# Wide tiles: the ring of weights' sums 64 bytes further, low parts ahead, both pairs of a step in a row, and four banks a pair

## The chip, the cores and the metric

The kernel runs on one core of a Trainium2 chip. The metric is the device time of one execution in microseconds; the median of three runs of the kernel before is 1164.0 us (1163.58 to 1164.37).

## The reference

Block-causal attention over 8 batches and 8 heads (sequence 576, head size 64, blocks of 64), and behind it a SwiGLU feed-forward on the 4608 tokens, all in float32:

```
scores = where(block_i >= block_j, (q @ k.T) / sqrt(64), -1e9)
x      = softmax(scores) @ v            # heads side by side: 4608 x 512
g      = x @ w_gate                     # 512 x 1536
val    = x @ w_val                      # 512 x 1536
out    = (g * sigmoid(g) * val) @ w_out # 1536 x 512
```

## The kernel before

**Precision.** A matmul's operands are float32 values split into a high and a low part. A product is three matmuls into one sum in PSUM: high by high, high by low, low by high.

**Order of the work.** The program first collects tasks (engine, cost in us, rank, buffers, what they wait for). A planner, `in_order()`, then plays them through on all engines at once with these costs and takes, whenever an engine is free, the task of least rank that is ready and finds a buffer slot. Slots whose tag is in `IN_TURN` are handed out in the order of the program. The order that comes out is the order of the instructions on every engine; what they wait for on the chip is set by the buffers that they share. Where the planner sees TensorE without work for over 0.3 us, `keep_busy` puts small filler matmuls there (64 columns, L1887 before, L1902 after).

**Stages.** Attention of the eight batches and the feed-forward of the finished tokens run next to each other. Twelve tiles of 256 tokens go the ordinary way: a step is gate and value products of two chunks of 128 hidden columns (48 matmuls of 128x256 at L1148: the gate's weights g_even and g_odd for the even and the odd chunk, the value's v_all), then twelve matmuls of 128x512 for the product with w_out (L1240 to L1242, "down").

**Wide tiles.** The last three tiles have 512 tokens each, from 870 us on. Gate and value products go by a scheme of seven products of half-size blocks in place of eight. A tile has six steps, each for two chunks: a gate `Pair` g and a value `Pair` v, both of 7 products of 6 matmuls of 128x256 (L1510). Products "1", "2" and "4" use the resident weights, "5", "6", "7" and "3" sums of weights, which `mix_weights` has worked out and stored in HBM (mix_d) during the attention. They are loaded from there into a ring of six slots in the buffer sc, four entries a pair, each entry by two DMAs of 128 KB (L1485, issued on SP's queue); an entry can be loaded once the product that used its slot is over. A pair's products stand in two PSUM tiles "at" of two banks each.

**Recombination.** ScalarE copies product "1" out of PSUM (s1, L1546); VectorE adds in four instructions at L1541: o1 (s1 to "2" and "6"), o2 ("7"), o3 ("5"), o4 ("3" and "4"). They write the pair's c, in the second sc buffer. Then `gates` (tanh on ScalarE, L1583; silu on VectorE, L1586) and `values` (product of gate and value on VectorE, L1599; its high part on ScalarE, L1602; its low part on VectorE, L1605). `bring` prepares the next tile's input blocks on VectorE and ScalarE meanwhile.

**Down chunks.** A step yields two chunks for `down` (12 matmuls of 128x512, L1628 to L1630, into the PSUM tiles po and gv, which add over a whole tile). They are put off: `owed` keeps them, and `give()` issues one of the previous step. So a step before reads: gate pair, gates, one down chunk of the step before, value pair, the other chunk, values.

## Time and profile before

| what | value |
|---|---|
| runs, median (lowest to highest) | 1164.0 us (1163.58 to 1164.37) |
| the profiled execution | 1164.27 us, span 1162.4 us, mean granted clock 0.993 |
| TensorE busy, 0 to 150 us | 142.84 of 150.00 us |
| TensorE busy, 150 to 870 us | 714.63 of 720.00 us |
| TensorE busy, 870 us to the end | 285.50 of 292.40 us |
| VectorE busy in these three | 122.73, 641.70 and 170.87 us |
| share of the DMA engines' time, 870 us to the end | 0.67, 211 GB/s |

A timeline row reads: start, how long the group lasted, engine, line, operation, output<-inputs by the program's names, tile shape, number of instructions, and in brackets the idle time before it and what ended that. A matmul's own duration (0.39 to 0.50 us) is longer than the distance to the next one, since matmuls are pipelined: what counts is the distance from start to start. A windows row gives the window, its length, busy time (and instructions) of PE, PEld (TensorE's weight loads), DVE (VectorE), ACT (ScalarE) and POOL, then the granted clock, the DMA share and GB/s. In the wide tiles the inputs' tiles carry the names of buffers that the attention no longer needs (qk, parts, mx, sr, xu, v, xhl).

### The profile page before, as it was taken

The numbers are of one execution on the slowest core, as the hardware profiler recorded it, in microseconds if no ns is written. First come the engines' busy times: TensorE is split into PE (matmuls) and PEld (weight loads), VectorE is DVE, ScalarE is ACT, GpSimd is POOL, SyncE is SP. The second block draws the span as 40 slices with busy tenths as digits, with TensorE's granted clock in tenths as the row PEclk, the third lists the DMA queues.
The fourth block names the chain that finished last, engine by engine and source line by source line (L and its number), as shares of the span: only waits on it lengthen the run. The fifth ranks groups of instructions, "written<-read, shape, count | busy, mean of one in ns | idle before, by whom it ended". The sixth has DMA issues, their size and how long they took to land.

```text
span 1162.4 us, 23307 instructions
## 1 busy us (share of the span) xinstructions
PE 1143.0 (98%) x8780; PEld 1008.5 (87%) x8780; DVE 935.3 (80%) x1540; ACT 580.2 (50%) x1052; POOL 324.7 (28%) x141
## 2 busy tenths in 40 slices
PE   8999999999999999999999999999999999999998
PEld 7778788889888888888888988988998999999996
DVE  4998898888898899998999999987665567556554
ACT  5889776755554465445565555554332224222222
POOL 3213101163644523454554345445100000000000
PEclk8999999999999999999999999999999999999999
DMA  7857766866666468767676668774577667766762
GB/s 193 225 147 210 198 189 229 214 186 183 151 191 168 142 186 222 202 188 203 195 190 184 179 176 239 203 216 159 177 226 246 220 205 232 226 205 222 241 209 99
DMA packets 328624, 228.97 MB, mean 197 GB/s; under 512 B 200064, under 2 KB 297616, under 8 KB 328512
## 3 DMA queue, kind: packets, MB, share of 16 engines
q1 hardware_dynamic: 325936, 226.77, 67.7%
q8 instruction: 69, 1.13, 0.4%
q10 hardware_dynamic: 2576, 0.72, 0.3%
q14 instruction: 43, 0.35, 0.1%
HBM read 190.45 MB, written 36.96 MB: 196 GB/s over the span
## 4 chain that ended last, share of the span: by engine, by line
PE 38%; DVE 10%; issue 2%; ACT 1%; POOL 1%; DMA 0%; DVEq 0%; ACTq 0%; POOLq 0%
PE at L1510 15%; PE gv L1148 8%; DVE mx L749 2%; DVE sc L779 2%; PE po L1240 2%; PE po L1241 1%; PE po L1242 1%; PE po L1628 1%; PE po L1629 1%; PE po L1630 1%; PE gv L1628 1%; PE gv L1629 1%; PE gv L1630 1%; PE at L861 1%; DVE hhl L1198 1%
## 5 line engine op out<-in xcount | busy, mean ns | idle before, releaser
L912 POOL PARTITION_ALL_REDUCE mx<-mx x48 | 181.1, 3826 | 183.8 <-DVE mx L749 175.8
L753 POOL PARTITION_ALL_REDUCE mx<-mx x80 | 143.1, 1832 | 305.9 <-DVE mx L749 191.7
L1148 PE MATMUL gv<-xhl,v_all 128*128 128x256 f32 x1728 | 221.1, 279 | 0.7 <-DVE t L1190 0.5
L1148 PEld LDWEIGHTS gv<-xhl,v_all 128*128 128x128 f32 x1728 | 208.2, 188 | 5.4 <-issue 1.9
L1541 DVE TENSOR_TENSOR sc<-sc,at 128x512 f32<-128x512 f32 (+1 forms) x144 | 89.3, 620 | 90.4 <-ACT sc L1546 53.5
L779 DVE TENSOR_TENSOR sc<-sc,mx 128x640 f32<-128x640 f32 (+6 forms) x168 | 127.1, 800 | 2.2 <-POOL mx L753 2.1
L749 DVE TENSOR_TENSOR mx<-mx,sc 128x128 f32<-128x128 f32 (+2 forms) x180 | 124.4, 703 | 1.5 <-ACT sc L783 0.3
L1148 PE MATMUL gv<-xhl,g_even 128*128 128x256 f32 x864 | 120.3, 284 | 2.0 <-DVE t L1185 2.0
L783 ACT ACTIVATE sc<-sc 128x1024 f32<-128x1024 f32 (+3 forms) x104 | 105.8, 1033 | 30.8 <-DVE sc L779 30.0
L1148 PEld LDWEIGHTS gv<-xhl,g_even 128*128 128x128 f32 x864 | 110.4, 189 | 8.8 <-DVE t L1185 2.2
L1148 PE MATMUL gv<-xhl,g_odd 128*128 128x256 f32 x864 | 115.8, 280 | 0.0
L1148 PEld LDWEIGHTS gv<-xhl,g_odd 128*128 128x128 f32 x864 | 107.2, 189 | 2.0 <-issue 1.2
L1240 PE MATMUL po<-wo,hhl 128*128 128x512 f32 x252 | 103.6, 411 | 0.7 <-ACT ob L1267 0.7
L1241 PE MATMUL po<-wo,hhl 128*128 128x512 f32 x252 | 98.8, 392 | 0.0
L1242 PE MATMUL po<-wo,hhl 128*128 128x512 f32 x252 | 98.5, 391 | 0.0
L861 PE MATMUL at<-sc,v 128*64 128x320 f32 (+4 forms) x888 | 94.3, 362 | 1.6 <-ACT parts L463 1.2
L709 ACT ACTIVATE sc<-at 128x576 f32<-128x576 f32 (+1 forms) x96 | 76.6, 835 | 31.5 <-PE at L692 31.4
L861 PEld LDWEIGHTS at<-sc,v 128*64 128x64 f32 x888 | 60.1, 137 | 36.1 <-ACT sc L783 2.0
L692 PE MATMUL at<-parts,qk 64*128 64x288 f32 (+4 forms) x864 | 73.9, 310 | 1.7 <-DVE qk L674 1.2
L692 PEld LDWEIGHTS at<-parts,qk 64*128 64x128 f32 x864 | 62.3, 185 | 14.7 <-issue 5.0
L1195 ACT CAST hhl<-t 128x512 fp32r<-128x512 f32 x72 | 44.8, 623 | 58.5 <-DVE t L1190 37.6
L1198 DVE TENSOR_TENSOR hhl<-t,hhl 128x512 fp32r<-128x512 f32 x72 | 62.7, 871 | 10.8 <-ACT hhl L1195 10.7
(238 smaller groups left out, 2037.3 us busy)
## 6 DMA issues: line engine op xcount, KB each, us to landing
wo<-wo_d SPq DMA_DIRECT2D x164, 512.0 KB
sc<-mix_d SPq DMA_DIRECT2D x288, 128.0 KB
mix_d<-wo SPq DMA_DIRECT2D x48, 256.0 KB
out_dram<-ob SPq DMA_DIRECT2D x35, 256.0 KB
v<-in_v_dram SPq DMA_DIRECT2D x64, 128.0 KB
rt<-r_d SPq DMA_DIRECT2D x128, 64.0 KB
qk<-in_q_dram SPq DMA_DIRECT2D x112, 72.0 KB
qk<-in_k_dram SPq DMA_DIRECT2D x104, 72.0 KB
```

The lines of the kernel that those rows point to most:

```text
L692: nc.tensor.matmul(ps[0][:, x, o : o + w], lhsT=part(1, kl)[own(x), c * P : (c + 1) * P], rhs=part(0, ql)[own(x), qs : qs + w], start=n == ...
L749: nc.vector.tensor_tensor(into, prev, of(c), op)
L753: nc.gpsimd.partition_all_reduce(m, m, channels=P, reduce_op=bass_isa.ReduceOp.max)
L779: nc.vector.tensor_tensor(piece(c), scores_of(c), m, ALU.subtract)
L783: nc.scalar.activation(x, x, AF.Exp)
L861: nc.tensor.matmul(ps[0][own(x), 1 - i if sums else i, q0 - s0 : s1 - s0], lhsT=ones if sums else vt[0][:, 2 * lane + c, own(x)], rhs=sc[0 ...
L912: nc.gpsimd.partition_all_reduce(m, m, channels=P, reduce_op=bass_isa.ReduceOp.add)
L1148: nc.tensor.matmul(o, lhsT=part[:, d], rhs=xs[d][1][x][:, 0:w], start=first, stop=last)
L1240: nc.tensor.matmul(po, lhsT=hi, rhs=whi, start=i + y == 0, stop=False)
L1241: nc.tensor.matmul(po, lhsT=hi, rhs=wlo, start=False, stop=False)
L1242: nc.tensor.matmul(po, lhsT=lo, rhs=whi, start=False, stop=i + y == NFC - 1)
L1510: nc.tensor.matmul(self.spot(name), lhsT=a, rhs=b, start=n == 0, stop=n == len(every) - 1)
```

## The change

1. The first sc buffer is 16 words longer, and the ring's views begin 16 words (64 bytes) further in it (`shifted`). The views that used the second sc buffer (`plain`, `four`) are written anew for its new shape; they hold the same bytes.
2. `product` takes several names. The gate's "12" issues its four matmuls of the low weights first, then the eight of the high ones.
3. A pair's order is "12", "6", "75", "34" in place of "15", "26", "7", "34", and the ring's entries come in the order 6, 7, 5, 3. The four banks of a pair are four `Part`s ("bank") of the two PSUM tiles, handed out in turn.
4. In a step, `v.issue()` stands ahead of the first `give()`: gate pair, value pair, then both down chunks.
5. In `mix_weights` the sums for the value weights are one VectorE instruction of 128x512 in place of two of 128x256 (twelve times), and the planner is given that cost.

```diff
--- before.py
+++ after.py
@@ -301,7 +301,7 @@
-    pool_of(const, "sc", 2, now=([([P, 2, WS], F32)], None), late=([([P, 6, 2 * XT], F32R)], None))
+    pool_of(const, "sc", 2, now=([([P, 2, WS], F32)], None), late=([([P, 6 * 2 * XT + 16], F32R)], None))
@@ -1287,8 +1287,12 @@
 
                 def whole(which=which, i=i, c=c, sums=sums):
                     to = sums[0].rearrange("p (d y f) -> p d y f", d=2, y=2)
+                    if which:
+                        hi, lo = (v_all[x][:, c::2, i * P : (i + 2) * P].bitcast(F32) for x in range(2))
+                        nc.vector.tensor_tensor(to.rearrange("p d y f -> p d (y f)"), hi, lo, ALU.add)
+                        return
                     for y in range(2):
-                        hi, lo = (w_at(which, x, i + y)[:, c :: 2].bitcast(F32) for x in range(2))
+                        hi, lo = (w_at(which, x, i + y)[:, c::2].bitcast(F32) for x in range(2))
                         nc.vector.tensor_tensor(to[:, :, y], hi, lo, ALU.add)
 
                 def mixes(sums=sums):
@@ -1312,7 +1316,7 @@
-                t = add("DVE", 2 * dve_us(2 * P), R, whole, [*w_done.values(), *early], [sums, mix], True)
+                t = add("DVE", dve_us(DM) if which else 2 * dve_us(2 * P), R, whole, [*w_done.values(), *early], [sums, mix], True)
@@ -1333,7 +1337,11 @@
         def cut(b, k, x):
             return b, lambda b: (b[x][:, k, 0:w], b[x][:, k, w:W])
 
-        sc = [cut(b, k, 0) for b in parent["sc"] for k in range(6)]
+        def shifted(b, k):
+            at = 16 + k * W
+            return b, lambda b: (b[0][:, at : at + w], b[0][:, at + w : at + W])
+
+        sc = [shifted(parent["sc"][0], k) for k in range(6)]
@@ -1347,17 +1355,17 @@
...
+        ats = [Buf("at") for _ in range(2)]
+        banks = [(b, lambda b, k=k: b[0][:, k]) for b in ats for k in range(2)]
+        slots["bank"] = [[None, None] for _ in banks]
         RING = 6
         AT = {"5": 3, "6": 0, "7": 1, "3": 2}
         slots["ring"] = [[None, None] for _ in range(RING)]
@@ -1473,11 +1481,11 @@
             def __init__(self, j, i, which, xs, ready, E, rank):
                 self.E, self.rank, self.i, self.which = E, rank, i, which
                 self.xs, self.ready = xs, ready
-                self.ps = [Buf("at") for _ in range(2)]
+                self.ps = [Part("bank", banks) for _ in range(4)]
                 self.c = Part("value" if which else "gate", four[which : which + 1])
                 n, stored = mixed[which, i]
                 self.ring, self.loads = {}, {}
-                for name in "5673":
+                for name in "6753":
                     x = Part("ring", sc[0:RING])
 
                     def load(n=n, b=AT[name], x=x):
@@ -1489,34 +1497,42 @@
                     self.ring[name] = x
                     self.loads[name] = dma(E, 2.6e5, load, stored, [x], 2)
 
-            def product(self, name, low_first=False):
-                hw, lw = {}, {}
-                which, i = self.which, self.i
-                for c in range(2):
-                    if name in "124":
-                        y, d = {"1": (0, c), "2": (0, 2 + c), "4": (1, 2 + c)}[name]
-                        hw[c], lw[c] = (w_at(which, x, i + y)[:, d] for x in range(2))
-                    else:
-                        v = self.ring[name].view()
-                        hw[c], lw[c] = (v[x][:, c * P : (c + 1) * P] for x in range(2))
-                x = [self.xs[XN[name], c].view() for c in range(2)]
-                every = [[(lw[c], x[c][0]), (hw[c], x[c][0]), (hw[c], x[c][1])] for c in range(2)]
+            def product(self, names, low_first=False):
+                every = []
+                for name in names:
+                    which, i = self.which, self.i
+                    some, o = [], self.spot(name)
+                    for c in range(2):
+                        if name in "124":
+                            y, d = {"1": (0, c), "2": (0, 2 + c), "4": (1, 2 + c)}[name]
+                            hi, lo = (w_at(which, x, i + y)[:, d] for x in range(2))
+                        else:
+                            hi, lo = (v[:, c * P : (c + 1) * P] for v in self.ring[name].view())
+                        x = self.xs[XN[name], c].view()
+                        some.append([(o, lo, x[0]), (o, hi, x[0]), (o, hi, x[1])])
+                    every.append(some)
                 if low_first:
-                    every = [[a for a, _, _ in every]] + [[b, c] for _, b, c in every]
+                    order = [three[0] for some in every for three in some]
+                    order += [p for some in every for three in some for p in three[1:]]
                 else:
-                    every = [[b, c, a] for a, b, c in every]
-                every = sum(every, [])
-                for n, (a, b) in enumerate(every):
-                    nc.tensor.matmul(self.spot(name), lhsT=a, rhs=b, start=n == 0, stop=n == len(every) - 1)
+                    order = [three[k] for some in every for three in some for k in (1, 2, 0)]
+                left, seen = {}, set()
+                for o, _, _ in order:
+                    left[id(o)] = left.get(id(o), 0) + 1
+                for o, a, b in order:
+                    left[id(o)] -= 1
+                    nc.tensor.matmul(o, lhsT=a, rhs=b, start=id(o) not in seen, stop=not left[id(o)])
+                    seen.add(id(o))
 
             def spot(self, name):
-                k, bank, o = {
-                    "1": (0, 0, 0), "5": (0, 0, 1), "2": (0, 1, 0), "6": (0, 1, 1), "7": (1, 0, 0), "3": (1, 1, 0), "4": (1, 1, 1)
-                }[name]
-                return self.ps[k][0][:, bank, o * w : (o + 1) * w]
+                k, o = {"1": (0, 0), "2": (1, 0), "6": (1, 1), "7": (2, 0), "5": (2, 1), "3": (3, 0), "4": (3, 1)}[name]
+                return self.ps[k].view()[:, o * w : (o + 1) * w]
+
+            def pair_of(self, k):
+                return self.ps[k].view().rearrange("p (k n) -> p k n", k=2)
 
             def on_pe(self, names):
-                bufs, after = [self.ps["734".find(names[0]) >= 0]], []
+                bufs, after = [*dict.fromkeys(self.ps[{"1": 0, "2": 1, "6": 1, "7": 2, "5": 2}.get(n, 3)] for n in names)], []
                 for name in names:
                     bufs += [self.xs[XN[name], c] for c in range(2)]
                     after += [self.ready[XN[name], c] for c in range(2)]
@@ -1525,18 +1541,17 @@
                         after.append(self.loads[name])
 
                 def products():
-                    for name in names:
-                        self.product(name, name == "1" and not self.which)
+                    self.product(names, "1" in names and not self.which)
 
                 return on_pe(up_us(6 * len(names)), self.rank, products, bufs, after=after, stage="up")
 
...
-                t15 = self.on_pe("15")
-                s1 = add("ACT", act_us(w, True), E, out_of_psum, [t15], [p0, c])
-                self.t = t26 = self.on_pe("26")
+                self.t = t12 = self.on_pe("12")
+                s1 = add("ACT", act_us(w, True), E, out_of_psum, [t12], [pa, c])
+                t6 = self.on_pe("6")
                 o1 = op(
-                    W, [t26, s1], [p0],
+                    W, [t6, s1], [pb],
                     lambda: c.view()[:, 0:2],
                     lambda: c.view()[:, 2:3].to_broadcast([P, 2, w]),
-                    lambda: p0[0][:, 1].rearrange("p (k n) -> p k n", k=2),
+                    lambda: self.pair_of(1),
                 )
-                t7 = self.on_pe("7")
-                o2 = op(w, [t7, o1], [p1], lambda: at(2), lambda: at(1), lambda: self.spot("7"))
+                t75 = self.on_pe("75")
+                o2 = op(w, [t75, o1], [pc], lambda: at(2), lambda: at(1), lambda: self.spot("7"))
                 o3 = op(
-                    W, [o2, t15], [p0],
+                    W, [o2], [pc],
                     lambda: c.view()[:, 1::2],
                     lambda: c.view()[:, 1:3],
                     lambda: self.spot("5").rearrange("p (k n) -> p k n", k=1).to_broadcast([P, 2, w]),
                 )
                 t34 = self.on_pe("34")
                 o4 = op(
-                    W, [t34, o3], [p1],
+                    W, [t34, o3], [pd],
                     lambda: c.view()[:, 1:3],
                     lambda: c.view()[:, 1:3],
-                    lambda: p1[0][:, 1].rearrange("p (k n) -> p k n", k=2),
+                    lambda: self.pair_of(3),
                 )
                 self.done = [o3, o4]
@@ -1684,8 +1699,8 @@
                     chain["down"] = []
                     first[0] = False
                 before = gates(g)
+                v.issue()
                 give()
-                v.issue()
                 give()
                 hidden = values(v, before)
@@ -1758,7 +1773,7 @@
 
 
     IN_TURN = set(
-        "qk v parts sc mx xu sr gv hhl t xt rt xhl ring gate value plain".split()
+        "qk v parts sc mx xu sr gv hhl t xt rt xhl ring gate value plain bank".split()
     )
 
     def in_order():
```

TensorE at the start of a gate pair in the third tile, first before, then after (g_even_73 is the low part, g_even_72 the high part, sc the ring, at_0_161 and at_0_213 the two PSUM tiles):

```order
L1630 MATMUL gv_0_189<-wo_0_2044,hhl_1_108 128x512
L1510 MATMUL at_0_161<-qk_0_8859,g_even_73 128x256 x2
L1510 MATMUL at_0_161<-qk_0_8859,g_even_72 128x256 x4
L1510 MATMUL at_0_161<-qk_0_8977,sc_0_8653 128x256 x6
L1510 MATMUL at_0_161<-qk_0_8859,g_even_72 128x256 x2
L1510 MATMUL at_0_161<-qk_0_8859,g_even_73 128x256
L1510 MATMUL at_0_161<-qk_0_8977,g_even_72 128x256 x2
L1510 MATMUL at_0_161<-qk_0_8977,g_even_73 128x256
L1510 MATMUL at_0_161<-parts_0_9000,sc_0_8653 128x256 x3
L1510 MATMUL at_0_161<-parts_1_9001,sc_0_8653 128x256 x3
```

```order
L1645 MATMUL gv_0_189<-wo_0_2044,hhl_1_108 128x512
L1524 MATMUL at_0_161<-qk_0_8857,g_even_73 128x256 x3
L1524 MATMUL at_0_161<-qk_0_8978,g_even_73 128x256
L1524 MATMUL at_0_161<-qk_0_8857,g_even_72 128x256 x6
L1524 MATMUL at_0_161<-qk_0_8978,g_even_72 128x256 x2
L1524 MATMUL at_0_161<-parts_0_8989,sc_0_8626 128x256 x3
L1524 MATMUL at_0_161<-parts_1_8990,sc_0_8626 128x256 x3
L1524 MATMUL at_0_213<-parts_0_8960,sc_0_8626 128x256 x3
L1524 MATMUL at_0_213<-parts_1_8961,sc_0_8626 128x256 x3
L1524 MATMUL at_0_213<-qk_0_8978,sc_0_8626 128x256 x6
```

The four matmuls of the low part stand together at the start, and no ring product stands between "1" and "2".

TensorE where that gate pair ends, before and after:

```order
L1510 MATMUL at_0_213<-mx_0_8953,sc_0_8653 128x256 x6
L1510 MATMUL at_0_213<-mx_0_9009,g_odd_68 128x256 x2
L1510 MATMUL at_0_213<-mx_0_9009,g_odd_69 128x256
L1510 MATMUL at_0_213<-mx_0_9009,g_odd_68 128x256 x2
L1510 MATMUL at_0_213<-mx_0_9009,g_odd_69 128x256
L1628 MATMUL po_0_262<-wo_0_2083,hhl_0_109 128x512
L1629 MATMUL po_0_262<-wo_0_2083,hhl_0_109 128x512
```

```order
L1524 MATMUL at_0_213<-mx_0_8941,sc_0_8626 128x256 x6
L1524 MATMUL at_0_213<-mx_0_9009,g_odd_68 128x256 x2
L1524 MATMUL at_0_213<-mx_0_9009,g_odd_69 128x256
L1524 MATMUL at_0_213<-mx_0_9009,g_odd_68 128x256 x2
L1524 MATMUL at_0_213<-mx_0_9009,g_odd_69 128x256
L1524 MATMUL at_0_161<-qk_0_8857,v_all_70 128x256 x2
L1524 MATMUL at_0_161<-qk_0_8857,v_all_71 128x256
L1524 MATMUL at_0_161<-qk_0_8857,v_all_70 128x256 x2
```

Before, the down chunk follows the gate pair; now the value pair does (v_all). It takes 18 matmuls ("12" and "6") until the tile at_0_213 is written again.

In the second step of the second and of the third tile the value pair's last two groups stand like this on TensorE after the change (the ring products are "75", then "34"):

```order
L1524 MATMUL at_0_213<-parts_0_8960,sc_0_8626 128x256 x3
L1524 MATMUL at_0_213<-parts_1_8961,sc_0_8626 128x256 x3
L1524 MATMUL at_0_213<-qk_0_8978,sc_0_8626 128x256 x6
L1902 MATMUL po_0_262<-ones 64x64 x4
L1524 MATMUL at_0_213<-mx_0_8941,sc_0_8626 128x256 x6
L1524 MATMUL at_0_213<-mx_0_9009,v_all_70 128x256 x2
L1524 MATMUL at_0_213<-mx_0_9009,v_all_71 128x256
```

Four filler matmuls stand ahead of "34". On VectorE in the second step of the second tile, before (L1586 is the gate's silu, L1541 o1 to o4 of the value pair, L1599 its product with the gate) and after (L1601 the silu, L1556 o1 to o4 of the value pair):

```order
L1586 SCALAR_TENSOR_TENSOR t_0_111<-t_0_111,sc_0_8840 128x512 [waits Activation_49]
L1586 SCALAR_TENSOR_TENSOR t_0_977<-t_0_977,sc_0_8840 128x512 [waits Activation_49]
L1541 TENSOR_TENSOR sc_0_8840<-sc_0_8840,at_0_161 128x512 [waits Activation_49]
L1541 TENSOR_TENSOR sc_0_8840<-sc_0_8840,at_0_213 128x256 [waits DVE_49,PE_49]
L1541 TENSOR_TENSOR sc_0_8840<-sc_0_8840,at_0_161 128x2x256 [waits DVE_49]
L1541 TENSOR_TENSOR sc_0_8840<-sc_0_8840,at_0_213 128x512 [waits DVE_49]
L1599 SCALAR_TENSOR_TENSOR t_0_111<-t_0_111,sc_0_8840 128x512 [waits DVE_49]
```

```order
L1601 SCALAR_TENSOR_TENSOR t_0_111<-t_0_111,sc_0_8825 128x512 [waits Activation_49]
L1601 SCALAR_TENSOR_TENSOR t_0_977<-t_0_977,sc_0_8825 128x512 [waits Activation_49]
L1556 TENSOR_TENSOR sc_0_8825<-sc_0_8825,at_0_161 128x512 [waits Activation_49]
L1556 TENSOR_TENSOR sc_0_8825<-sc_0_8825,at_0_213 128x256 [waits DVE_49,PE_49]
L1556 TENSOR_TENSOR sc_0_8825<-sc_0_8825,at_0_213 128x2x256 [waits DVE_49]
L1556 TENSOR_TENSOR sc_0_8825<-sc_0_8825,at_0_213 128x512 [waits DVE_49,PE_49]
```

In these two steps o4 of the value pair has a wait for TensorE of its own beside that of o2, where in the other steps o2 alone waits, for the pair's last matmul: here o2 and o3 stand ahead of "34" in the program, and all three work on at_0_213. They also stand behind the two silus.

13 lines of the change are left out of this document (5 added, 8 removed).

## The prediction

> **What bounds the kernel now.** I read the busy shares first, then the windows, then what TensorE waits for in the wide stage.
>
> ```profile
> PE 1143.0 (98%) x8780; PEld 1008.5 (87%) x8780; DVE 935.3 (80%) x1540; ACT 580.2 (50%) x1052; POOL 324.7 (28%) x141
> 870.00:1162.40 292.40, 285.50 (x1978) 264.84 (x1976) 170.87 (x287) 69.52 (x138) 0.00 (x0) 1.00 0.67 211
> 150.00:870.00 720.00, 714.63 (x5601) 630.01 (x5600) 641.70 (x1008) 390.12 (x685) 287.52 (x101) 1.00 0.68 192
> PE at L1510 <- DVE sc L1541: 1.3, 1, 1.3
> ```
>
> TensorE is busy 98% of the span. In the wide stage (870 us to the end) the granted clock is 1.00 (the figure ahead of the DMA share) and the one wait for the recombination is 1.3 us long, the last row. So the stage's time is the sum of TensorE's intervals from start to start, and there are two ways to change it: shorter intervals, or new waits. VectorE is busy 171 of 292 us there and is not the bound, but its chains end waits.
>
> One step of the wide stage is a gate pair (42 matmuls at L1510), a down chunk (12 at L1628 to L1630), a value pair and a second down chunk. TensorE's timeline of one step:
>
> ```profile
> 1042.58 0.86 PE L1510 MATMUL at<-xhl,g_even 128*128 128x256 f32 x6
> ...
> 1047.54 0.40 PE L1628 MATMUL po<-wo,hhl 128*128 128x512 f32 x1
> ...
> 1050.29 0.87 PE L1510 MATMUL at<-xhl,v_all 128*128 128x256 f32 x6
> 1050.99 0.87 PE L1510 MATMUL at<-xhl,sc 128*128 128x256 f32 x6
> ...
> 1053.84 0.88 PE L1510 MATMUL at<-v,sc 128*128 128x256 f32 x6
> 1054.56 0.84 PE L1510 MATMUL at<-xu,v_all 128*128 128x256 f32 x6
> 1055.24 0.40 PE L1628 MATMUL po<-wo,hhl 128*128 128x512 f32 x1
> ```
>
> From start to start the gate pair takes 4.96 us, the down chunk 2.75, the value pair 4.95: with the second chunk, 15.41 us a step. The product from the ring ("sc") that starts at 1053.84 takes 0.72 for six, 120 ns each; the last one from the resident weights v_all takes 0.68, 113 ns. Both have the same shape, so the place of the weights matters. In the allocation of the built kernel the ring lies at multiples of 128 bytes, as do the moving operands; v_all, g_odd and the high parts of g_even lie 64 bytes beside such multiples, and g_even's low part on them.
>
> An ordinary step before the wide stage has the same 128x256 matmuls without a ring:
>
> ```profile
> 837.73 1.54 PE L1148 MATMUL gv<-xhl,g_even 128*128 128x256 f32 x12
> 839.11 1.52 PE L1148 MATMUL gv<-xhl,g_odd 128*128 128x256 f32 x12
> 840.47 2.88 PE L1148 MATMUL gv<-xhl,v_all 128*128 128x256 f32 x24
> 843.19 0.40 PE L1240 MATMUL po<-wo,hhl 128*128 128x512 f32 x1
> ```
>
> The 24 of v_all take 2.72 us, 113.3 ns each. The g_even group, whose four low parts go first, takes 1.38 for 12, 0.02 over 12 times 113.3, and nothing is written to g_even in that time. I read the ring's 120 ns as a matter of address and not of the transfers that fill it.
>
> **The change, part by part.** *The ring's shift and the low parts first.* If all ring products run at 113.3 ns, a value pair takes 42 x 0.1133 = 4.76 us and a gate pair, with the 0.02 for its low parts, 4.78. The step becomes 4.78 + 4.76 + 2 x 2.75 = 15.04 us against 15.41: 0.37 less, times 18 steps, **6.7 us gained**. Bounds: at best the same; at worst only the resident products gain, and the 24 ring products of 36 pairs keep their 120 ns: 24 x 36 x 0.0067 = 5.8 us of the gain are gone. I take the full gain, since g_odd and v_all, 64 bytes off, show it. In the Trainium skill, "SBUF — State Buffer", section "Who interferes with whom", TensorE has one read port for the moving operand and another, independent one for the weights, and waits on nobody. By that rule the shift would gain nothing, and the sum would be 5.8 us higher. The 0.72 against 0.68 us of the rows shows that equal matmuls do differ with the weights' place, so I follow the row.
>
> *The order "12", "6", "75", "34", both pairs in a row.* No matmul is added. But the value pair now stands right behind the gate pair, with no down chunk between them, and its "75" goes into the PSUM tile of two banks from which VectorE has yet to take the gate's products 7, 5, 3 and 4. The four banks are parts of two tiles, and the built program's waits go by tile: "75" of the value pair waits for the last addition (o4) of the gate pair, and the first addition into that tile (o2) waits for the gate's last matmul. What that chain takes is in the trace, in the chain that ended last and in the timeline near the end:
>
> ```profile
> 886.50 0.43 DVE sc L1541
> 886.96 0.70 DVE sc L1541
> 887.65 0.14 issue
> 887.79 3.81 PE at L1510 x30
> ...
> 1147.00 0.84 PE L1510 MATMUL at<-mx,v_all 128*128 128x256 f32 x6
> 1147.68 0.40 PE L1628 MATMUL po<-wo,hhl 128*128 128x512 f32 x1
> 1147.88 1.87 DVE L1541 TENSOR_TENSOR sc<-sc,at 128x256 f32<-128x256 f32 x3 [1.03 <-PE at L1510]
> ```
>
> The last matmul of a pair starts 0.11 before 1147.68, at 1147.57; o2 starts at 1147.88, 0.31 later; o2, o3 and o4 take 1.87; from the end of an addition to the matmul that it releases pass 0.14 us (887.65 to 887.79). Together 2.32 us. Meanwhile TensorE has "12" and "6" of the value pair: from the gate's last matmul to the start of "75" 19 intervals of 113.3 ns, 2.15 us. It stands for 0.17 us. A wait also has an aftermath:
>
> ```profile
> 656.24 3.09 PE L1148 MATMUL gv<-xhl,v_all 128*128 128x256 f32 x24 [0.54 <-DVE t L1190]
> 659.25 1.02 PE L692 MATMUL at<-parts,qk 64*128 64x448 f32 x10
> ```
>
> These 24 matmuls after a wait take 3.01 us where the 24 at 840.47 took 2.72: 0.29 more. Part of that may lie in the passage to the other matmuls at 659.25, so I take 0.2. Each such wait then costs 0.37 us. There is one in each of 18 steps, and one more at the start of the first tile, whose first step has no down chunks behind it: 19 x 0.37 = **7.0 us lost**. Bounds: 0, if the additions are over sooner than these rows say by 0.17 us; and 19 x (0.17 + 0.29) = 8.7. I take 7.0, since the two rows for the chain agree to 0.01 us. Behind the waiting "75" stand "34" and both down chunks; nobody else waits for them, since the down chunks' results go out only at a tile's end.
>
> *Two longer waits.* In the value pairs of the second step of the second and the third tile, the order sets o2 and o3 of that same pair ahead of its "34", in the same tile: "34" has to wait for o3, and o3 stands on VectorE behind the gate's silu (L1586). The rows for that:
>
> ```profile
> 894.34 1.41 DVE L1541 TENSOR_TENSOR sc<-sc,at 128x512 f32<-128x512 f32 x2
> 895.84 1.15 ACT L1583 ACTIVATE t<-sc 128x512 f32<-128x512 f32 x2 [3.47 <-DVE sc L1541]
> 896.50 1.30 DVE L1586 SCALAR_TENSOR_TENSOR t<-t,sc 128x512 f32<-128x512 f32 x2 [0.76 <-ACT t L1583]
> L1541 DVE TENSOR_TENSOR sc<-sc,at x144: 415/686/690, 876.4 to 1149.1; 128x512 f32<-128x512 f32 x108, 128x256 f32<-128x256 f32 x36
> ```
>
> o4 of a gate ends at 894.34 + 1.41 = 895.75 and the two silus at 896.50 + 1.30 = 897.80, 2.05 later. Then o1, o2, o3: 0.69 + 0.42 + 0.69 with three times 0.02 between, 1.86, and 0.14 to the matmul: "34" starts 4.05 us after o4 of the gate. Without that wait it would start after 0.14 and the twelve matmuls of "75" at 117 ns and the slow start, some 1.6 us. So 2.4 us of standing and 0.1 for the new start, 2.5 us, twice: **5.0 us lost**. Bounds: 2.0 and 3.0 each.
>
> *What goes away.* The wait at 887.79 and the small ones behind the last value pair:
>
> ```profile
> 885.62 0.84 PE L1510 MATMUL at<-mx,v_all 128*128 128x256 f32 x6
> 887.79 0.94 PE L1510 MATMUL at<-qk,g_even 128*128 128x256 f32 x6 [1.33 <-DVE sc L1541]
> ...
> 1150.20 0.39 PE L1630 MATMUL gv<-wo,hhl 128*128 128x512 f32 x1
> ...
> 1152.24 0.39 PE L1628 MATMUL po<-wo,hhl 128*128 128x512 f32 x1
> ```
>
> The six at 885.62 need 0.68 and the next would start at 886.30, not 887.79: 1.5 us gained, as that gate's "12" writes a tile that is free by then. At the end, the matmul at 1152.24 is the fourth after 1150.20 + 0.23, so without waits it would start at 1151.12: 1.1 us gained, because two down chunks, 5.5 us, now lie between the last value pair and the chunks that need its result, where one chunk of 2.75 lay. **2.6 us gained.**
>
> *The sums of weights.* Twelve pairs of 128x256 additions become twelve of 128x512, and the planner, given another duration, sets the attention's matmuls in another order from the middle of the attention on. The windows bound it:
>
> ```profile
> 500.00:700.00 200.00, 197.48 (x1577) 173.30 (x1574) 191.68 (x297) 108.99 (x190) 94.63 (x33) 1.00 0.70 190
> ```
>
> VectorE is nearly full there (191.68 of 200), but TensorE too (197.48), and over 150 to 870 us TensorE idles 5.4 us in all. The twelve instructions saved are worth little while TensorE stays full; the new order may win some of those 5.4 us or add to them. I count nothing, with 2 us either way, a third of them and a little more.
>
> **Sum.** -6.7 + 7.0 + 5.0 - 2.6 = +2.7 us. The profiled execution took 1164.27 us (1162.4 of span and 1.9 around it), 0.27 above the median of the runs, 1164.0. So the forecast is 1164.0 + 2.7 = **1166.7 us**.
>
> **The rivals.** *A, the waits cost next to nothing.* If the additions finish 0.17 us sooner, or "75" starts 0.17 us later because "12" and "6" still run at 117 to 120 ns, the stops and their aftermath vanish: 7.0 us less, 1159.7 us, faster. For it: 0.17 us is a small difference of two sums of 2.2. Against it: what lengthens "12" and "6" takes as much from the gain. *B, the two long waits are absent or short.* That takes 5.0 us off, 1161.7 us or, with half of them, 1164.2: no change. Against it: they are in the order of the instructions. *C, the ring's products stay at 120 ns.* Then 5.8 us of the gain are lost; "12" and "6" take 6 x 0.0067 = 0.04 longer, which shortens 19 waits to 0.33: 0.8 back, 1171.7 us, slower. For it: the transfers that fill the ring go on next to it, in both kernels; against it: g_even's row. It is also what the Trainium skill's rule of two ports (page and section above) comes to. *D, the ring runs dry.* Entries 3 and 4 of a value pair now reuse the slots of the gate's first two, 48 matmuls or 5.4 us ahead, where a down chunk lay between. The stage moves 211 GB/s at a DMA share of 0.67, and a pair's entries are 1 MB, so it should hold; if each third entry came 0.5 us late in 18 steps, 9 us more, 1175.7. *E, the earlier order.* 2 us either way on top of any of them.
>
> **How the numbers follow.** I give the forecast, with its own range 1164.5 to 1169, 0.45; A 0.2; B 0.2; C 0.1; D 0.05. 0.2% of 1164.0 is 2.3 us, about what a measurement of this kernel can tell from no change. Slower (over 1166.3): 0.29 of the forecast's cases, C, D and 0.01 of B, 0.45. The same: 0.16 of the forecast, 0.14 of B and 0.05 of A, 0.35. Faster (under 1161.7): 0.15 of A and 0.05 of B, 0.20. The range reaches down to A's 1159.7 and up to the forecast with the upper price of the waits and the earlier order against it, 1166.7 + 1.7 + 1.5: 1159.5 to 1170.
>
> **What would show it.** In TensorE's waits from 870 us on, 19 new entries of L1524 for VectorE's L1556 of about 0.1 to 0.2 us, and two of over 2 us. In a step, six ring matmuls in 0.68 us where 0.72 stood, and after the short wait 0.70 to 0.71. No idle row near 887 and none after the last value pair. The wide stage starting within 2 us of where it did, near 870 us. The forecast is wrong if L1556 is missing among the waits (A), if only the two long ones are missing (B), if ring products still take 0.72 (C), if a wait names the transfer sc<-mix_d (D), or if the stage starts further off (E).

## The result, and the profile after

The changed kernel took **1175.65 us** (median of four runs, 1174.48 to 1177.83) where the kernel before took 1164.18: a ratio of 1.0101 (95% interval 1.0084 to 1.0119), 11.5 us slower. The forecast was 1166.7 us in a range of 1159.5 to 1170: the right sign, and far too small.

The profiled execution (1177.83 us, span 1176.0) tells at once that most of it did not happen in the wide stage. TensorE's timeline there begins with the first of these rows (columns: start, length, engine, line, tiles, count); before, the stage began at 870.56 us.

```profile
882.18 1.54 PE L1524 MATMUL at<-qk,g_even 128*128 128x256 f32 x12
```

So 11.62 us were lost ahead of the wide stage, and the stage itself took 1176.02 - 882.18 = 293.84 us in place of 291.88: 1.96 more. (Their sum, 13.6, is 2 us above the difference of the medians, since the profiled execution was the slowest of the four.) The windows of the changed kernel that answer to those shown of before (busy us of PE, PEld, DVE, ACT, POOL, then granted clock, DMA share, GB/s):

```profile
150.00:870.00 720.00, 705.50 (x5527) 620.87 (x5526) 635.66 (x979) 387.62 (x679) 288.09 (x101) 1.00 0.67 189
500.00:700.00 200.00, 192.52 (x1518) 169.81 (x1517) 189.55 (x279) 106.67 (x186) 87.55 (x31) 0.98 0.66 183
```

TensorE's idle time between 150 and 870 us grew from 5.4 to 14.5 us, and the granted clock of 500 to 700 us fell to 0.98. What TensorE waited for, from 150 to 870 us (first two rows) and from 870 us on (last two):

```profile
PE gv L1148 <- DVE t L1185: 8.8, 4, 4.9
PE at L861 <- ACT sc L721: 2.5, 2, 1.6
...
PE at L1524 <- DVE sc L1556: 3.1, 2, 1.6
PE at L1524 <- DMA sc<-mix_d: 2.0, 2, 1.1
```

L1185 is the silu of the ordinary tiles on VectorE; the next gate product needs the PSUM bank that it reads. Before, all waits for it came to 2.0 us. The longest one now is 4.9 us. VectorE and GpSimd around it:

```profile
520.31 0.94 DVE L1310 TENSOR_TENSOR wo<-ob,wo 128x512 fp32r<-128x512 f32 x1
521.17 0.28 DVE L1301 TENSOR_TENSOR ob<-ob 128x128 f32<-128x128 f32 x1
521.49 2.69 DVE L1302 TENSOR_TENSOR ob<-ob 128x128 f32<-128x128 f32 x1
524.22 0.29 DVE L1303 TENSOR_TENSOR ob<-ob 128x128 f32<-128x128 f32 x1
524.54 0.29 DVE L1304 TENSOR_TENSOR ob<-ob 128x128 f32<-128x128 f32 x1
524.75 0.68 DVE L1185 SCALAR_TENSOR_TENSOR t<-t,gv 128x512 f32<-128x512 f32 x1
525.54 0.69 DVE L1190 SCALAR_TENSOR_TENSOR t<-t,gv 128x512 f32<-128x512 f32 x1
526.14 2.08 DVE L674 TENSOR_TENSOR qk<-sr,qk 128x576 fp32r<-128x576 f32 x1
...
521.43 7.25 POOL L912 PARTITION_ALL_REDUCE mx<-mx  x2
```

L1301 to L1304 are the additions of `mix_weights`. They stand ahead of the silu, and the second one takes 2.69 us in place of 0.29, from the moment that GpSimd's all-reduce starts. The same place in the kernel before:

```profile
516.88 0.64 DVE L1185 SCALAR_TENSOR_TENSOR t<-t,gv 128x512 f32<-128x512 f32 x1
...
521.05 0.29 DVE L1298 TENSOR_TENSOR ob<-ob 128x128 f32<-128x128 f32 x1
521.37 2.50 DVE L1299 TENSOR_TENSOR ob<-ob 128x128 f32<-128x128 f32 x1
...
521.12 7.25 POOL L912 PARTITION_ALL_REDUCE mx<-mx  x2
```

There an addition is held up just as long, but the silu is over by then. The wait also has a price of its own behind it (a window of the changed kernel, and TensorE's timeline):

```profile
526.00:531.50 5.50, 5.50 (x28) 5.50 (x27) 2.83 (x3) 0.49 (x1) 4.65 (x2) 0.50 0.64 189
```

```profile
525.49 2.93 PE L1148 MATMUL gv<-xhl,g_even 128*128 128x256 f32 x12 [4.91 <-DVE t L1185]
528.21 2.76 PE L1148 MATMUL gv<-xhl,g_odd 128*128 128x256 f32 x12
530.77 3.32 PE L1148 MATMUL gv<-xhl,v_all 128*128 128x256 f32 x24
534.02 1.06 PE L692 MATMUL at<-parts,qk 64*128 64x288 f32 x12
```

The granted clock is 0.50 up to 531.5 us. From start to start the twelve g_even products take 2.72 us where the step before the change that the prediction shows at 837.73 took 1.38, the g_odd ones 2.56 where it took 1.36, and the 24 of v_all, most of them at the full clock again, 3.25 where it took 2.72: about another 3 us. The Trainium skill says in "TensorE: Matmul & The Clock Gate", Part 1, that a stretch of about 3.4 us without work halves TensorE's clock until it has worked as long again. The wait of 4.91 us and the 0.50 agree with it; the half clock lasted longer here, 6.0 us of work, and a run below has it behind a wait of only 2.70 us.

In the wide stage, one step of the third tile after the change:

```profile
1071.27 1.54 PE L1524 MATMUL at<-qk,g_even 128*128 128x256 f32 x12
...
1076.05 1.52 PE L1524 MATMUL at<-qk,v_all 128*128 128x256 f32 x12
1077.41 1.73 PE L1524 MATMUL at<-parts,sc 128*128 128x256 f32 x12
1078.98 0.84 PE L1524 MATMUL at<-qk,sc 128*128 128x256 f32 x6
1079.66 0.84 PE L1524 MATMUL at<-mx,sc 128*128 128x256 f32 x6
...
1081.02 0.40 PE L1643 MATMUL po<-wo,hhl 128*128 128x512 f32 x1
...
1086.49 0.40 PE L1524 MATMUL at<-qk,g_even 128*128 128x256 f32 x2
```

Six ring products take 0.68 us (1078.98 to 1079.66) where they took 0.72. The gate pair takes 4.78 us. The row of twelve at 1077.41 is "6" and "7" of the value pair (the profile joins them, since their inputs have the same names); it takes 1.57 us where twelve products need 1.36. The step takes 15.22 us, 15.21 in most steps. From the starts of the gate pairs, the steps of the wide stage:

| step | before, us | after, us |
|---|---|---|
| first of the first tile | 17.23 | 15.25 |
| second of the first tile | 16.10 | 17.47 |
| first of the second tile | 15.42 | 16.91 |
| second of the second and of the third tile | 15.41 | 17.69, 17.75 |
| the other twelve | 15.41 | 15.21 (two 15.31) |
| the last, up to the start of the last matmul | 21.78 | 20.41 |

The two rows of 17.7 are the two long waits. The second of the first and the first of the second tile contain a wait for the ring's transfers (2.0 us in the two by the view of waits).

### The profile page after: what moved, and what is told of

Its sections match the earlier page's. It is cut to its first block, busy times and chain, and to the rows that moved or that the text cites. A ratio compares the mean times of both kernels' runs of the same rounds, so it can differ in the third digit from the quotient of the medians.

```text
span 1176.0 us, 23325 instructions
## 1 busy us (share of the span) xinstructions
PE 1142.5 (97%) x8796; PEld 1006.1 (86%) x8796; DVE 935.8 (80%) x1528; ACT 578.3 (49%) x1052; POOL 325.3 (28%) x141
## 4 chain that ended last, share of the span: by engine, by line
PE 74%; DVE 15%; DMA 4%; ACT 3%; issue 2%; SPq 1%; POOL 1%; DVEq 0%; ACTq 0%
PE gv L1148 25%; PE at L1524 14%; PE at L861 7%; PE po L1240 4%; PE at L692 4%; PE po L1241 4%; PE po L1242 4%; DVE mx L749 2%; DVE sc L779 2%; PE po L1644 1%; PE po L1643 1%; PE po L1645 1%; PE gv L1644 1%; DVE hhl L1198 1%; PE gv L1645 1%
## 5 line engine op out<-in xcount | busy, mean ns | idle before, releaser
L1148 PE MATMUL gv<-xhl,v_all 128*128 128x256 f32 x1728 | 221.4, 279 | 1.9 <-DVE t L1190 1.8
L1148 PEld LDWEIGHTS gv<-xhl,v_all 128*128 128x128 f32 x1728 | 208.6, 188 | 6.5 <-DVE t L1190 2.7
L1556 DVE TENSOR_TENSOR sc<-sc,at 128x512 f32<-128x512 f32 (+1 forms) x144 | 89.2, 620 | 67.5 <-PE at L1524 43.0
L1148 PE MATMUL gv<-xhl,g_even 128*128 128x256 f32 x864 | 121.5, 285 | 8.9 <-DVE t L1185 8.8
L779 DVE TENSOR_TENSOR sc<-sc,mx 128x640 f32<-128x640 f32 (+6 forms) x168 | 123.7, 779 | 5.2 <-POOL mx L753 5.2
L1148 PEld LDWEIGHTS gv<-xhl,g_even 128*128 128x128 f32 x864 | 111.0, 190 | 16.7 <-DVE t L1185 10.3
L749 DVE TENSOR_TENSOR mx<-mx,sc 128x128 f32<-128x128 f32 (+2 forms) x180 | 117.8, 669 | 1.3
L1148 PE MATMUL gv<-xhl,g_odd 128*128 128x256 f32 x864 | 116.0, 280 | 0.0
L1148 PEld LDWEIGHTS gv<-xhl,g_odd 128*128 128x128 f32 x864 | 107.3, 190 | 2.0 <-issue 1.2
L709 ACT ACTIVATE sc<-at 128x576 f32<-128x576 f32 (+1 forms) x96 | 76.5, 836 | 32.5 <-PE at L692 32.4
L1198 DVE TENSOR_TENSOR hhl<-t,hhl 128x512 fp32r<-128x512 f32 x72 | 69.9, 970 | 14.6 <-ACT hhl L1195 14.5
L692 PE MATMUL at<-parts,qk 64*128 64x288 f32 (+4 forms) x864 | 73.8, 310 | 0.6 <-DVE qk L674 0.5
L692 PEld LDWEIGHTS at<-parts,qk 64*128 64x128 f32 x864 | 62.2, 185 | 12.8 <-issue 3.5
L1617 ACT CAST hhl<-t 128x512 fp32r<-128x512 f32 x36 | 22.4, 622 | 101.3 <-DVE t L1614 60.2
```

What stands on the lines that cost most here:

```text
L692: nc.tensor.matmul(ps[0][:, x, o : o + w], lhsT=part(1, kl)[own(x), c * P : (c + 1) * P], rhs=part(0, ql)[own(x), qs : qs + w], start=n == ...
L749: nc.vector.tensor_tensor(into, prev, of(c), op)
L779: nc.vector.tensor_tensor(piece(c), scores_of(c), m, ALU.subtract)
L1148: nc.tensor.matmul(o, lhsT=part[:, d], rhs=xs[d][1][x][:, 0:w], start=first, stop=last)
```

## The experiments

Theory O says that the loss ahead of the wide stage comes from the order that the planner made of the new cost of the sums; rival W, that the wide tiles' edits disturb what is ahead of them. Theory S says that the wide stage gained by the shift and lost by its new waits.

**The parts of the change alone.** First the changed kernel with the old sums of weights:

```diff
-                    if which:
-                        hi, lo = ...  # one addition of 128x512
-                        return
...
-                t = add("DVE", dve_us(DM) if which else 2 * dve_us(2 * P), R, whole, ...
+                t = add("DVE", 2 * dve_us(2 * P), R, whole, ...
```

> The changed kernel with the sums of weights as before (two additions of 128x256, and the planner's old cost for them); the wide tiles as changed. Theory O (the new order of the attention's matmuls, which the planner made from the new cost, took most of the loss): the wide stage starts near 870.6 us as before, the wide stage keeps its +2.0 us, so about 1166.2 us (1165 to 1167.5). Rival W (the wide tiles' edits, their buffers or their slots disturb the stages ahead): still about 1175.

Measured: 1166.09 us, ratio to before 1.0024 (1.0009 to 1.0038). Then the other way round, the kernel before with the new sums and their cost, and nothing else:

> The kernel before with only the sums of weights changed (one addition of 128x512 and its cost). Theory O: it loses what the changed kernel lost ahead of the wide stage, 9 to 12 us: about 1174 us, with a wait of about 5 us of L1148 for VectorE near 520 us. Rival W: about 1164.

Measured: 1174.17 us, ratio 1.0092 (1.0074 to 1.0109); its wide stage is step for step that of before from the second step on, and its longest wait is 5.1 us for the silu L1185. Theory O holds, rival W falls: the sums alone cost 11.0 us, the wide edits alone 2.9 (together 13.9 against the 11.5 of the whole change, whose interval reaches from 9.8 to 13.9).

Is it the instruction or the order? The changed kernel, with the new instruction and the old cost:

```diff
-                t = add("DVE", dve_us(DM) if which else 2 * dve_us(2 * P), R, whole, ...
+                t = add("DVE", 2 * dve_us(2 * P), R, whole, ...
```

> The changed kernel with the one addition of 128x512, but the planner is given the old cost, so the order of the instructions ahead of the wide stage is as before. Theory O: about 1166 us, like the run with the old sums, or up to 1 us less since VectorE has twelve instructions less. Rival I (the instruction itself, not the order, delays VectorE): about 1175.

Measured: 1163.08 us, ratio 1.0001 (0.9990 to 1.0012). The order, then; rival I falls. With the old order the same instruction loses nothing, and by the medians it saves some 3 us (1166.09 to 1163.08, though the ten runs of each overlap). The 0.07 us that the planner was told to take off for each of the twelve is all that separates this kernel from the changed one, some 12 us slower at 1175.65. A third cost, between the two:

```diff
-                t = add("DVE", dve_us(DM) if which else 2 * dve_us(2 * P), R, whole, ...
+                t = add("DVE", 0.64 if which else 2 * dve_us(2 * P), R, whole, ...
```

> The changed kernel, where the planner is told 0.64 us for the addition of 128x512, between the changed kernel's 0.602 and the old 0.672. That gives a third order of the attention. Theory L (the orders are a lottery on this scale: each places other work ahead of what TensorE waits for): a time that is neither near 1175.65 nor near 1163.1, anywhere from 1160 to 1180. Rival G (the planner's new cost is worse because it is too low: VectorE's addition takes 0.69): between the two, about 1169.

Measured: 1175.10 us, ratio 1.0105 (1.0085 to 1.0125). Rival G falls. Theory L's letter missed too, since the time is that of the changed kernel; but it is another order with other waits (its longest for L1185 is 2.5 us, and its wide stage starts at 883.46 us). Two orders out of three lose about the same amount, in different places.

**Why the new order is slow.** Theory M: the additions of the sums stand ahead of silus that TensorE waits for. The first test leaves three of each four additions out, in both orders:

```diff
                     nc.vector.tensor_tensor(a22, a21, a22, ALU.add)
-                    nc.vector.tensor_tensor(a21, a11, a21, ALU.subtract)
-                    nc.vector.tensor_tensor(a11, a22, a11, ALU.subtract)
-                    nc.vector.tensor_tensor(a12, a12, a11, ALU.subtract)
```

> The kernel before with only the sums of weights changed, and with three of the four 128x128 additions of each sum left out (the wide tiles' output is not the reference's); the planner is still given their cost, so the order is that of the run with the changed sums. Theory M (in the new order these additions stand on VectorE ahead of the silu that TensorE waits for, near 518 us, and one of them is held up for 2.4 us while GpSimd's all-reduce runs): the wait of 5.4 us there shrinks to about 2, and the time lies 4 us or more below the 1174.2 of the full sums, less what the same removal brings in the old order. Rival Q (the order of the attention's matmuls is slow by itself): the wait and the distance of 10 to 11 us to the old order stay.

> The kernel before with three of the four 128x128 additions of each sum left out (the wide tiles' output is not the reference's), in the old order. What VectorE gains there by itself: 72 additions of 0.29 us, 21 us and the time for which some of them are held up, but TensorE waits only 5.4 us in all between 150 and 870 us, so 0 to 4 us less than before, 1159 to 1163.

Measured: 1154.26 us in the new order (ratio 0.9926, 0.9905 to 0.9947) and 1155.81 in the old one (0.9933, 0.9913 to 0.9954). The whole distance of 11 us between the orders is gone, so TensorE's new order isn't slow by itself: rival Q falls. The old order gained 6 us, more than the 0 to 4 expected. All that TensorE still waits for at L1148 from 150 to 860 us, in the new order without these additions (the row of the old order without them is the same):

```profile
PE gv L1148 <- DVE t L1185: 0.7, 1, 0.7
```

This leaves open whether the place of the additions counts or their sum (rival V). So the next kernels do all the work of the new order and move nothing but silus on VectorE (and one copy of ScalarE that waits for such additions): a step behind the planner puts a silu that stands right behind additions of the sums ahead of them. Nine silus at first:

```diff
+    order = silus_first(order)  # a silu ahead of the mix_weights tasks right in front of it
```

> The kernel before with only the sums of weights changed, in the new order that follows from it, except that on VectorE nine silus that stand right behind additions of the sums are put ahead of them; TensorE's order is that of the run with the changed sums, and all work is done. Theory M (the new order loses because these additions, some of them held up by GpSimd's all-reduce, stand ahead of silus that TensorE waits for): the wait of 5.4 us near 518 us falls under 2.5, and the time from 1174.2 to 1169 or less, if it is all of the loss to about 1164. Rival V (VectorE has simply too much to do in the new order, wherever the additions stand): 1172 to 1175.

Measured: 1170.86 us, ratio 1.0058 (1.0043 to 1.0073), 3.3 us less than the 1174.17. The wait near 518 us is 2.7 us where it was 5.1, a little over the expected 2.5. The order there had stayed as it was, with four additions ahead of the silu, since the rule would not pass another task that uses the same buffer. A second kernel moves that one silu too, and nothing else; the first one was run again beside it:

> As the run with nine silus moved ahead, and one more: the silu near 518 us, which that run left behind four additions of the sums (one of them held up to 2.69 us). Nothing else differs on any engine. Theory M at this place: the wait of 3.0 us near 518 us falls under 0.5, and with what the granted clock loses behind it the time falls by 2.5 to 5 us against the run with nine silus, to about 1167. Rival V: the wait moves to the next thing that VectorE owes, and the time stays.

> The run with nine silus moved ahead once more, on the same chip as the run with ten, for the comparison: 1170.9 by the first look, 1169.5 to 1172.

Measured: 1166.84 us with ten silus (ratio 1.0050, 1.0034 to 1.0067) and 1170.92 with nine (1.0078, 1.0065 to 1.0091). That place with nine, on TensorE and in a window:

```profile
515.48 2.88 PE L1148 MATMUL gv<-xhl,v_all 128*128 128x256 f32 x24
521.06 2.93 PE L1148 MATMUL gv<-xhl,g_even 128*128 128x256 f32 x12 [2.70 <-DVE t L1185]
523.79 1.90 PE L1148 MATMUL gv<-xhl,g_odd 128*128 128x256 f32 x12
525.53 2.99 PE L1148 MATMUL gv<-xhl,v_all 128*128 128x256 f32 x24
...
521.00:524.00 3.00, 2.94 (x13) 2.94 (x14) 2.90 (x4) 0.06 (x1) 3.00 (x1) 0.51 0.90 194
```

And with ten, on VectorE and on TensorE (L1190 is the silu's product with the value):

```profile
515.71 0.67 DVE L1185 SCALAR_TENSOR_TENSOR t<-t,gv 128x512 f32<-128x512 f32 x1
516.30 2.41 DVE L1301 TENSOR_TENSOR ob<-ob 128x128 f32<-128x128 f32 x1
...
512.73 2.88 PE L1148 MATMUL gv<-xhl,v_all 128*128 128x256 f32 x24
516.43 1.68 PE L1148 MATMUL gv<-xhl,g_even 128*128 128x256 f32 x12 [0.82 <-DVE t L1185]
517.95 1.57 PE L1148 MATMUL gv<-xhl,g_odd 128*128 128x256 f32 x12
520.35 3.09 PE L1148 MATMUL gv<-xhl,v_all 128*128 128x256 f32 x24 [0.82 <-DVE t L1190]
```

One silu put ahead of four additions gains about 4 us by the medians (1170.92 to 1166.84; two of the six runs with ten lie at 1170.4 and 1171.7, so the size is less sure than the sign). In the two profiles some 2.4 us of it lie at this place: the v_all products ahead of it start 2.75 us apart (515.48 and 512.73), those behind it 5.18 (525.53 and 520.35). Most of the 2.75 comes from a place that the edit does not touch, where TensorE waits 1.4 to 1.6 us for ScalarE in both: from 460 to 485 us the granted clock is 0.93 with nine and 1.00 with ten. The addition is held up as before (2.41 us), but the gate product waits 0.82 us in place of 2.70, and the clock stays up; the next instruction that the addition delays, L1190, costs another 0.82, so the expected "under 0.5" missed. Theory M holds at this place, rival V does not. Against their own runs of before, the new order costs 11.0 us with no silu moved, 7.3 and 8.9 with nine, 4.9 with ten. The remaining 5 us were not taken apart (with ten, the longest waits are 1.6 us for ScalarE's L721, 1.6 for L1190 and 2.0 for L674), so for them theory M is not shown.

The rule is no gain by itself. Its control in the old order:

> The kernel before with the same rule on VectorE (eleven silus that stand right behind additions of the sums are put ahead of them), old sums and old order otherwise. Theory M: a gain here too where such a silu was waited for, but small, since the old order's longest wait of that kind is 2.0 us: 0 to 3 us less than before. Rival V: nothing.

Measured: 1166.38 us, ratio 1.0018 (1.0005 to 1.0032): slightly slower, with a wait of 3.0 us of the scores (L692) for ScalarE (L709) that was not there. What made ScalarE late was not followed. Both theories had expected no loss.

**The wide stage.** The shift alone, on the kernel before (the order of the instructions is the same on every engine):

```diff
-        sc = [cut(b, k, 0) for b in parent["sc"] for k in range(6)]
+        sc = [shifted(parent["sc"][0], k) for k in range(6)]
```

> The kernel before with the ring 64 bytes further and nothing else; every engine's instructions stand in the order of the kernel before. Theory A (address): the 24 ring products of a pair run at 113 ns where they took 120, so a step takes some 0.3 us less than 15.41 and the whole 5 to 6 us less, about 1157.5 us. Rival T (the ring's products are slow because transfers write next to them, or because of the products' order): a step stays at 15.41 us and the time within 1 us of before.

Measured: 1158.41 us, ratio 0.9948 (0.9931 to 0.9966). Its step is 15.13 us; two ring products in it:

```profile
1049.25 0.84 PE L1511 MATMUL at<-xhl,sc 128*128 128x256 f32 x6
1049.93 0.84 PE L1511 MATMUL at<-sr,sc 128*128 128x256 f32 x6
```

0.68 us for six, though the transfers into the ring go on as before: theory A holds, rival T falls, and this is the best of the edits that were run alone. The other way round, without the shift:

```diff
-            at = 16 + k * W
+            at = k * W
```

> The changed kernel with the old sums of weights and with the ring back at its old place; order of the products, banks and both pairs in a row as changed. Theory A: the ring's products take 120 ns again, 18 steps x 2 pairs x 24 x 0.0067 = 5.8 us, less what the later start of the value pair's second half saves in waits (18 x 0.04 to 0.17): 1169 to 1172 us against 1166.1 with the shift. Rival T: 1166.

Measured: 1168.23 us, ratio 1.0037 (1.0021 to 1.0052): some 2 us above the kernel with the shift and the old sums (1.0024), where 3 to 6 were expected. The ring's buffer is as long as in the changed kernel, so nothing but the ring has moved, and six of its products take 0.72 us again:

```profile
1063.66 0.88 PE L1520 MATMUL at<-qk,sc 128*128 128x256 f32 x6
1064.38 0.88 PE L1520 MATMUL at<-mx,sc 128*128 128x256 f32 x6
```

Its steps take 15.47 us where those with the shift take 15.21, but its second step takes 16.44 in place of 17.63, and no wait for the ring's transfers is left in it: with both pairs in a row, faster products run into the ring.

The down chunk between the pairs again, with the old sums:

```diff
                 before = gates(g)
-                v.issue()
                 give()
+                v.issue()
                 give()
```

> The changed kernel with the old sums of weights and with a down chunk between gate pair and value pair again, as before; shift, low parts ahead, products' order and banks stay. Theory S (in the wide stage the shift gains 0.37 us a step, and the waits that come from having both pairs in a row take it back): no wait for the recombination is left, a step takes 15.03 us against 15.41, the whole 18 x 0.37 = 6.7 us less than before, about 1157.5 us. Rival B (the new order of products and banks brings the waits): a step stays at 15.2 us or more, 1160.5 to 1164.

Measured: 1154.84 us, ratio 0.9935 (0.9910 to 0.9960). The step, by the rows of two gate pairs and of the value pair between:

```profile
1054.73 1.54 PE L1520 MATMUL at<-qk,g_even 128*128 128x256 f32 x12
...
1062.25 1.57 PE L1520 MATMUL at<-qk,v_all 128*128 128x256 f32 x12
1063.66 1.54 PE L1520 MATMUL at<-parts,sc 128*128 128x256 f32 x12
...
1069.83 0.40 PE L1520 MATMUL at<-qk,g_even 128*128 128x256 f32 x2
```

15.10 us in every step from the third on, and no wait for the recombination or the ring: theory S holds, rival B falls. The wide stage takes 284.59 us in this profile, 286.81 with the shift alone, and 293.63 with both pairs in a row (the run with the old sums): that one edit cost 9.0 us. Of the two long steps, the theory was that o2 and o3 stand ahead of "34":

```diff
                 t75 = self.on_pe("75")
-                o2 = op(w, [t75, o1], [pc], ...
+                t34 = self.on_pe("34")
+                o2 = op(w, [t75, t34, o1], [pc], ...
```

> The changed kernel with the old sums of weights, where the planner may issue o2 only behind the pair's products 3 and 4. Theory S (the long steps of the wide stage come from o2 and o3 standing ahead of 3 and 4 in one tile): the second step of the second and the third tile take 15.2 us where they took 17.7, and the whole is 4 to 5 us less than 1166.1, about 1161.5. Rival D (the long steps come from something else, the ring's loads or the silus): they stay, about 1166.

Measured: 1163.75 us, ratio 0.9999 (0.9985 to 1.0013), 2.3 us less than without that edit where 4 to 5 were expected. The two steps take 16.45 us in place of 17.7, not 15.2, so theory S has half of their length and the other half stays open: the planner still puts fillers there, and in this order "75" now waits for ScalarE's copy s1 in eight steps:

```profile
PE at L1520 <- ACT sc L1557: 2.7, 8, 0.3
```

**What beats both kernels.** The down chunk between the pairs in all steps but the last, the shift, the new products' order, and the one addition of 128x512 in the old order:

```diff
+                if j == len(TILES) - 1 and i >= NFC - 2:
+                    v.issue()
+                    give()
+                else:
+                    give()
+                    v.issue()
                 give()
```

> The changed kernel with a down chunk between gate pair and value pair in all steps but the last one, where both stand behind the value pair, and the one addition of 128x512 with the planner's old cost. By theory S and O the terms add up: 1154.8 (down chunk between), less 3.0 (the addition of 128x512 in the old order, from 1166.1 and 1163.1), less 1.1 (the waits behind the last value pair): about 1150.7 us (1149 to 1153). Rival: the terms overlap, 1154 or more.

Measured: 1154.50 us, ratio to before 0.9912 (0.9895 to 0.9929). The view of TensorE's waits shows none after 868 us, and its last step takes 20.41 us as in the changed kernel. Against the kernel with the chunk between in all steps its time is the same within what is measured, so the terms did not add up to 1150.7, as the rival had it. With the rule of the silus on top:

> The best kernel so far (down chunk between the pairs but in the last step, the addition of 128x512 in the old order), with the same rule on VectorE. Theory M: 0 to 3 us less than its 1154.5, as in the old order. Rival V: 1154.5.

Measured: 1156.22 us, ratio 0.9941 (0.9924 to 0.9957): no gain, and by the medians 1.7 us slower than without it.

## Why the prediction was wrong, point by point

**The step that failed** is "The sums of weights", with the sentence "I count nothing, with 2 us either way". It was +11.0 us (the sums alone). The bound was taken from the 5.4 us that TensorE idled before. That bounds what a new order can win, not what it can lose. What the runs showed in its place: the order made from the new cost puts additions of the sums ahead of silus that TensorE waits for. VectorE, busy 191.68 of 200 us in the window that the prediction itself quoted, has little room to catch up, and behind the longest of these waits TensorE ran at half its clock. With ten silus put ahead again the loss fell from 11.0 to 4.9 us; the cause of the rest stays open. Rival E had the right place and the wrong price, "2 us either way"; the sign named for it, a wide stage that starts more than 2 us off, is the one that showed (11.62 us).

**The ring's shift and the low parts:** right, a little too large. 113.3 ns, 4.78 us for the gate pair, a gain of 0.28 us a step by the shift alone and 0.31 with the order of the products, where 0.37 was counted: a down chunk between pairs keeps a little of its old cost (the value pair's first twelve take 1.41, not 1.36). By the Trainium skill's rule of two independent read ports ("SBUF — State Buffer", "Who interferes with whom"), which the prediction weighed, there would have been no gain; the shift alone gained 0.5% (ratio 0.9948).

**A wait in each step:** right in place, too dear. "75" of the value pair waits for o4 of the gate pair. In the step shown above, o4 ends at 1078.12 (the first row here, 1076.25 + 1.87), and "7" starts at 1078.17, where it would have started at 1078.09 (1077.41 and six times 0.1133):

```profile
1076.25 1.87 DVE L1556 TENSOR_TENSOR sc<-sc,at 128x256 f32<-128x256 f32 x3 [1.57 <-PE at L1524]
...
1078.17 0.97 PE L1524 MATMUL at<-parts,sc 128*128 128x256 f32 x6
```

The chain is as forecast, 1.87 us for o2 to o4. But only 0.05 us pass from its end to the matmul, not 0.14, so TensorE stands 0.08 us where 0.17 were counted; and the six that follow take 0.81 us in place of 0.68, an aftermath of 0.13 where 0.2 was taken from 24 products at 656 us. Together 0.21 (9.75 us for both pairs, against 4.78 + 4.76), not 0.37. The 19 new entries for L1556 that the prediction named as a sign are not in the view of waits, which has the two long ones alone: it counts idle time from the recorded end of a matmul, and that lies behind the place where the next one would start.

**The two longer waits:** right, 2.5 us each (17.69 and 17.75 against 15.21). In the second tile:

```profile
998.08 1.41 DVE L1556 TENSOR_TENSOR sc<-sc,at 128x512 f32<-128x512 f32 x2
1000.19 1.29 DVE L1601 SCALAR_TENSOR_TENSOR t<-t,sc 128x512 f32<-128x512 f32 x2 [0.70 <-ACT t L1598]
1001.40 1.93 DVE L1556 TENSOR_TENSOR sc<-sc,at 128x512 f32<-128x512 f32 x3
...
1003.38 0.97 PE L1524 MATMUL at<-v,sc 128*128 128x256 f32 x6 [1.55 <-DVE sc L1556]
```

o4 of the gate ends at 999.49 and "34" starts at 1003.38, 3.9 us later; 4.05 was forecast.

**What goes away:** 1.98 us in the first step and 1.37 in the last, 3.35 in all. Of that 0.2 each is what every step gained, so 2.95 stand against the 2.6 counted.

**Rival D, the ring runs dry,** got a chance of 0.05 and a price that was too high (9 us); it did happen, in two places, with waits of 2.0 us in all.

**The wide stage as a whole** came out at +2.0 us in the profile, where the sum had +2.7. That is luck: two errors cancel. By the table of steps, the shift less the wait in each step gained 0.20 us eighteen times, 3.6 us, where the sum had 6.7 gained and 7.0 lost. And the two steps with the ring's waits, for which the sum had nothing, grew by 3.3 us beyond that.

## What to carry to other kernels

Where a planner sets the order, a change of one cost is a change of every stage behind it. Cost it by the engine with the least room: compare the two orders on that engine around each instruction that the bounding engine waits for, and take the loss to be open upwards. Try an edit of the work and an edit of the cost apart; here the work cost nothing, and the order that came from its cost lost some 12 us (1163.08 to 1175.65). And of several edits to one stage, measure each alone: one of these (64 bytes) was worth 5 us, and another (both pairs in a row) took it back and more.

## What the runs showed of the hardware that was not expected

- An addition of 128x128 on VectorE with both operands in SBUF took 2.41 to 2.69 us in place of 0.29 when it met the start of GpSimd's all-reduce. L1190, which has one operand in PSUM, took its usual 0.69 us although it started 0.5 us into the second all-reduce (525.54), and L674 behind it, with both operands in SBUF, 2.08 where it took 0.75 alone. The Trainium skill, "SBUF — State Buffer", says in "Who interferes with whom" that a VectorE instruction with two SBUF inputs contends with a GpSimd instruction that reads SBUF, and in "SBUF: two separate sides" that the other is blocked for the whole instruction. The first agrees. The second does not quite: the addition was over at 524.18 and two more took 0.29 us each, while half of the 7.25 us, the first all-reduce, ends at about 525.1 in the profile (whose spans of GpSimd are rough).
- A wait of 4.91 us cost about 3 us more by the granted clock, 0.50 up to 531.5 us; a wait of 2.70 us was enough for a granted clock of 0.51 over the next three us.
- 64 bytes in the place of a matmul's weights are worth 6.7 ns of 120, at the same transfers, shapes and order, and are lost again when the ring alone goes back.
